# Value sums copied to SBUF before the softmax division, and the last stage's loads cut into paced pieces

## The chip, the cores and the metric

The kernel runs on one core of a Trainium2 chip. The metric is the device time of one execution in microseconds (us); three executions of the kernel before gave 1117.2, 1117.75 and 1119.46, so the median is 1117.75. Engines are called PE (TensorE), DVE (VectorE), ACT (ScalarE), POOL (GpSimd) and SP (SyncE, which issues all transfers here). PSUM is the memory that PE writes, in eight banks of 512 float32 columns; SBUF is the working memory.

## What is computed

One layer over a sequence of 2048 tokens of width 1024, batch 1, in bfloat16. Attention has 32 heads of width 32, and its result is multiplied, element by element, by a gate made from a two-layer network on the same normalized input.

```
xn  = layernorm(x)                                   # x: (1, 2048, 1024)
q, k, v = split(xn @ wqkv)                           # 32 heads of 32
p   = softmax(q @ k.T * 32 ** -0.5)                  # 2048 x 2048 per head
s   = concat_heads(p @ v) @ wo
y   = layernorm(xn)
g   = silu(gelu(y @ w1 + b1) @ w2 + b2)              # hidden width 3584
out = x + s * g
```

## The kernel before

The 32 heads are worked in eight groups of four (`HG = 8`), so that four heads fill the 128 partitions. Each group has eight blocks of 256 queries, and each block eight pairs of key tiles: 8 x 8 x 8 = 512 units of work. A unit (`unit`, line 921) is eight score matmuls on PE (line 932; one score group below), two exponentials of 128x1024 on ACT (line 941), the sum of the two key tiles on DVE (`PA`, line 944), and on PE eight small matmuls of the probabilities with V and four of `PA` with a tile of ones. The V products of a block gather in columns 0 to 255 of one PSUM bank and the softmax denominators in columns 256 to 511 of the same bank. `norm` (line 969) then divides: DVE transposes the denominators out of the bank (L971), takes reciprocals (L972), transposes these back and spreads them (L974), and multiplies the V sums, read from the bank, by them (L977). The bank is free for its next user after L977. Groups 0 to 6 write the result to a DRAM scratch (`o_scratch`, L1024); group 7 keeps it in `ot7`.

Everything else on PE is filler between the score groups, in four queues: `pro` (the first normalization and projections), `proj` (Q, K and V projections of the next group of heads), `mlp` (both layers of the network, whose weights stream in through rings of three `w1r` and four `w2r` tiles, L759 and L765, some 0.5 MB each), and `wo` (the output projection, one item for 128 tokens and 512 columns, eight matmuls over the eight head groups). The `wo` items need all heads: the seven stored groups come back from `o_scratch` into `big`, where the normalized input was (L997), and the weight `wo` goes where Q, K and the projection weights of finished groups were (L1000).

The order on every engine is made before launch by a planner (`_Plan.run`, line 78). It plays the program through with a cost for each instruction and gives each engine a fixed list; on the chip each engine follows its list and waits on semaphores. In the planner PE takes, at each free moment, the first of: a ready score group, the open V item, a filler item (`next_items`). A score group is put behind filler when the filler done so far lags the unit count (`paced`). A transfer costs its bytes at 210 GB/s behind all earlier ones, plus 1900 ns (`commit`, line 107). `proj` items fall due over 48 of the 64 units of a group.

So a piece of filler whose data the planner expects late is simply not in PE's list at that place, whether or not the data comes in time on the chip.

Line numbers of the changed kernel are 24 to 30 higher than those of the same code before (L932 is L956, L588 is L612, L765 is L789).

## Time and profile before

| what | value |
|---|---|
| median of 3 executions (lowest, highest) | 1117.75 us (1117.2, 1119.46) |
| profiled execution: its own time | 1117.59 us |
| its span, first to last instruction | 1115.4 us |
| busy: PE, ACT, DVE | 1038.8, 1034.9, 860.3 us |
| mean granted PE clock | 0.989 |

The profile gives for each engine how long it was busy. A PE row's end is modelled, and matmuls overlap, so a busy PE is not a PE at its peak. In a timeline row the first two numbers are start and length in us; the bracket gives the idle time of that engine just before, and which work ended it. A window row gives, for a stretch of the span, its length, the busy time of PE, of the weight loads (PEld), of DVE, ACT and POOL with the number of their instructions, then the granted PE clock (1.00 is full), the busy share of the DMA engines and their GB/s.

### The profile page before, as it was taken

The numbers are of one execution on the slowest core, as the hardware profiler recorded it, in microseconds if no ns is written. First come the engines' busy times: TensorE is split into PE (matmuls) and PEld (weight loads), VectorE is DVE, ScalarE is ACT, GpSimd is POOL, SyncE is SP. The second block draws the span as 40 slices with busy tenths as digits, with TensorE's granted clock in tenths as the row PEclk, the third lists the DMA queues.
The fourth block names the chain that finished last, engine by engine and source line by source line (L and its number), as shares of the span: only waits on it lengthen the run. The fifth ranks groups of instructions, "written<-read, shape, count | busy, mean of one in ns | idle before, by whom it ended". The sixth has DMA issues, their size and how long they took to land.

```text
span 1115.4 us, 34138 instructions
## 1 busy us (share of the span) xinstructions
PE 1038.8 (93%) x15238; PEld 669.1 (60%) x15305; DVE 860.3 (77%) x1570; ACT 1034.9 (93%) x1186; POOL 32.5 (3%) x42
## 2 busy tenths in 40 slices
PE   5898999999999899999999999999999997799997
PEld 4665476566766566557765666557666665466443
DVE  6699867787779776887779868976789777655775
ACT  4899989999999989999999999999999999868993
POOL 5600000000000000000000000000000000000000
PEclk9999999999999999999999999999999999799999
DMA  8345176233654356333574547333464547464333
GB/s 255 86 137 157 34 202 179 79 110 94 195 157 134 112 159 182 95 91 115 152 201 123 148 130 208 110 96 94 128 183 141 156 141 239 154 180 129 112 122 96
DMA packets 282380, 156.62 MB, mean 140 GB/s; under 512 B 23162, under 2 KB 271994, under 8 KB 282234
## 3 DMA queue, kind: packets, MB, share of 16 engines
q1 hardware_dynamic: 282234, 154.44, 47.9%
q8 instruction: 120, 1.97, 0.7%
q14 instruction: 26, 0.21, 0.1%
HBM read 142.35 MB, written 12.06 MB: 138 GB/s over the span
## 4 chain that ended last, share of the span: by engine, by line
ACT 57%; PE 37%; DVE 4%; POOL 1%; issue 1%; POOLq 0%; DMA 0%
ACT P L941 52%; PE ps L588 24%; PE ps L583 7%; PE ps L932 6%; ACT ut L815 3%; ACT gw L847 1%; POOL gw L724 1%; DVE PA L944 1%; DVE stats L710 0%; DVE nt L971 0%; DVE xb L807 0%; POOLq L1075 0%; ACT big L700 0%; DMA hT<-in_A_x_dram 0%; DVE hT L817 0%
## 5 line engine op out<-in xcount | busy, mean ns | idle before, releaser
L941 ACT ACTIVATE P<-ps 128x1024 bf16<-128x1024 f32 x1024 | 977.3, 1142 | 47.4 <-PE ps L932 44.9
L944 DVE TENSOR_TENSOR PA<-P 128x1024 bf16<-128x1024 bf16 x512 | 348.2, 688 | 134.7 <-ACT P L941 112.0
L588 PE MATMUL ps<-yT,w1r 128*128 128x256 bf16 x1792 | 232.3, 275 | 3.6 <-DVE xb L807 2.1
L588 PE MATMUL ps<-w2r,hT 128*128 128x256 bf16 x1792 | 224.6, 274 | 3.6 <-DVE hT L817 1.8
L588 PEld LDWEIGHTS ps<-yT,w1r 128*128 128x128 bf16 x1792 | 163.3, 98 | 60.3 <-issue 29.7
L588 PEld LDWEIGHTS ps<-w2r,hT 128*128 128x128 bf16 x1792 | 164.5, 98 | 52.1 <-issue 26.4
L583 PE MATMUL ps<-P,V 128*32 128x256 bf16 x4096 | 159.4, 276 | 0.8 <-DVE yT L1056 0.6
L588 PE MATMUL ps<-qk,big 128*128 128x256 bf16 (+1 forms) x718 | 120.3, 306 | 8.3 <-issue 1.9
L588 PE MATMUL ps<-big,qk 128*128 128x512 bf16 (+1 forms) x504 | 119.7, 367 | 8.5 <-issue 2.4
L932 PE MATMUL ps<-qk 32*128 32x256 bf16 x2048 | 102.3, 274 | 20.9 <-ACT P L941 19.8
L583 PE MATMUL ps<-PA,ones 128*32 128x256 bf16 x2048 | 118.0, 276 | 0.0
L932 PE MATMUL ps<-QKT 32*128 32x256 bf16 x2048 | 102.6, 275 | 16.1 <-ACT P L941 14.3
L583 PEld LDWEIGHTS ps<-P,V 128*32 128x32 bf16 x4096 | 102.0, 97 | 25.6 <-issue 9.5
L588 PEld LDWEIGHTS ps<-qk,big 128*128 128x128 bf16 x736 | 65.6, 98 | 48.4 <-issue 15.9
L815 ACT ACTIVATE ut<-ut 128x512 f32<-128x512 f32 x112 | 86.3, 773 | 2.9 <-DVE ut L813 2.9
L807 DVE TENSOR_TENSOR xb<-ps,b1T 128x512 bf16<-128x512 f32 x112 | 76.8, 685 | 15.6 <-PE ps L588 14.6
L817 DVE SCALAR_TENSOR_TENSOR hT<-ut,xb 128x512 bf16<-128x512 f32 x112 | 76.5, 684 | 8.4 <-ACT ut L815 8.3
L588 PEld LDWEIGHTS ps<-big,qk 128*128 128x128 bf16 x552 | 48.4, 99 | 57.1 <-issue 14.7
L932 PEld LDWEIGHTS ps<-qk 32*128 32x128 bf16 x2048 | 30.4, 92 | 84.4 <-ACT P L941 77.9
L932 PEld LDWEIGHTS ps<-QKT 32*128 32x128 bf16 x2048 | 30.4, 92 | 82.4 <-ACT P L941 75.3
L813 DVE SCALAR_TENSOR_TENSOR ut<-sq,xb 128x512 f32<-128x512 bf16 x112 | 76.9, 687 | 1.9
L583 PEld LDWEIGHTS ps<-PA,ones 128*32 128x32 bf16 x2048 | 53.1, 97 | 14.9 <-issue 13.3
(59 smaller groups left out, 460.6 us busy)
## 6 DMA issues: line engine op xcount, KB each, us to landing
w1r<-in_B_w_dram SPq DMA_DIRECT2D x112, 512.0 KB, 4.0
w2r<-in_B_w_dram SPq DMA_DIRECT2D x128, 448.0 KB, 4.3
qk<-in_A_wqkv_dram SPq DMA_DIRECT2D x16, 256.0 KB, 3.5
g_scratch<-gw SPq DMA_DIRECT2D x32, 128.0 KB, 2.7
o_scratch<-ot SPq DMA_DIRECT2D x56, 64.0 KB, 3.0
big<-o_scratch SPq DMA_DIRECT2D x7, 512.0 KB, 6.3
hT<-in_A_x_dram SPq DMA_DIRECT2D x10, 256.0 KB, 6.2
qk<-in_A_wqkv_dram SPq DMA_DIRECT2D x4, 512.0 KB, 4.3
```

The lines of the kernel that those rows point to most:

```text
L583: ins = e.matmul(dst(j), lhsT=lhsT(j), rhs=rhs(j), start=start, stop=stop, tile_position=(0, 32 * j), skip_group_check=True)
L588: return e.matmul(dst, lhsT=lhsT, rhs=rhs, start=start, stop=stop, skip_group_check=True)
L724: pool(lambda e, t=t: e.tensor_scalar(xnb[t % 4], xst[t], lnp[:, t, 1:2], lnp[:, t, 5:6], op0=ALU.mult, op1=ALU.add), 950, [XS(t), ("nb_", ...
L807: dve(lambda e: e.tensor_tensor(xb_t[i3][:].rearrange("p (k t) -> p k t", k=2), bank(it.bank).rearrange("p (k t) -> p k t", k=2), b1T[:, 2 ...
L813: dve(lambda e: e.scalar_tensor_tensor(ut_t[i3][:], sq_t[p % 2][:], 1.0 / GA, xb_t[i3][:], op0=ALU.add, op1=ALU.mult), c_f32(512), [("sq", ...
L815: act(lambda e: e.activation(ut_t[i3][:], ut_t[i3][:], ACT.Tanh, scale=GC * GA), c_act(512), [("ut", i3)], [("ut", i3)], 1)
L817: dve(lambda e: e.scalar_tensor_tensor(hT[:, hs].rearrange("p k t -> p (k t)"), ut_t[i3][:], 1.0, xb_t[i3][:], op0=ALU.add, op1=ALU.mult), ...
L847: act(lambda e: e.activation(zh_t[zi], z_t[zi], ACT.Tanh, scale=0.5), c_act(512), [("z", zi)], [("zh", zi)], 1)
L932: ins = e.matmul(bank(b0[j], kk * 256, (kk + 1) * 256), lhsT=QKT[sl][32 * j:32 * j + 32, 1, kb * 128:(kb + 1) * 128], rhs=QKT[sl][32 * j:3 ...
L941: x = act(lambda e, h=h: e.activation(P[pi][:, 2 * h:2 * h + 2].rearrange("p j k q -> p (j k q)"), ps[:, pr[h] * 1024:(pr[h] + 1) * 1024], ...
L944: pa = dve(lambda e: e.tensor_tensor(PA[ai][:], P[pi][:, :, 0, :], P[pi][:, :, 1, :], op=ALU.add), c_b16(1024), [("P", pi, 0), ("P", pi, 1 ...
```

## The change

Six edits go together.

- `norm` copies the V sums out of the bank into a new float32 tile `nv` (one more DVE instruction per block, 64 in all), right behind the transpose of the denominators, and multiplies from `nv`; the bank is free after this copy. Reciprocal, second transpose and product get a lower priority on DVE (2.2 in place of 1). To make room, the `PA` ring has seven tiles in place of eight.
- The seven transfers of 0.5 MB from `o_scratch` become 28 of 128 KB (seven groups by four quarters of the tokens); a quarter may start when its own quarter of the normalized input is no longer read.
- The one transfer of `wo` (2 MB) becomes eight of 256 KB, each waiting only for what lay in its place.
- These 36 pieces have the lowest priority in the planner and are issued only while its backlog of transfers is short; each is tied to the PE instruction that had last finished in the planner at that moment.
- The projections for the last group of heads fall due over 26 units in place of 48.
- `opens_at`: a filler item opens in the planner only when its later chunks will be ready too; a `wo` item only when all its data is planned.

```diff
--- before.py
+++ after.py
@@ -108,6 +108,11 @@
             e = o.eng
             o.start = t
             if e == "SP":
+                if o.prio >= 5:
+                    for x in reversed(order["PE"]):
+                        if x.fin <= t:
+                            o.deps[x] = True
+                            break
                 tf[e] = t + o.occ
                 state["bw"] = max(state["bw"], t) + o.nbytes / 210.0
                 o.fin = state["bw"] + 1900.0
@@ -137,6 +142,9 @@
                     pend[e].append(o)
             best = None
             bk = None
+            if e == "SP" and pend[e] and min(o.prio for o in pend[e]) >= 5 and state["bw"] > t + 1500:
+                wake(state["bw"] - 1400, e)
+                return None
             for o in pend[e]:
                 k = (o.prio, o.idx)
                 age = t - o.ready
@@ -188,6 +196,17 @@
             if pr is not None and "proj" not in out and (u >= pr.due - 12):
                 out.append("proj")
             return out
+
+        def opens_at(it, r):
+
+            off = 0.0
+            for c in it.chunks:
+                if c.left == 0:
+                    r = max(r, c.ready - off)
+                elif it.kind == "wo":
+                    return None
+                off += 1.2 * c.occ
+            return r
 
         def pe_step(t):
             cands = []
@@ -252,7 +271,10 @@
                             q.insert(heads["pro"], q.pop(k))
                         it = self.queues[n][heads[n]]
                         if it.chunks[0].left == 0:
-                            cands.append((max(bf[0], it.chunks[0].ready), 2, it.chunks[0], (it, bf[1], n)))
+                            r = opens_at(it, max(bf[0], it.chunks[0].ready))
+                            if r is None:
+                                continue
+                            cands.append((r, 2, it.chunks[0], (it, bf[1], n)))
                             if cands[-1][0] <= t:
                                 break
             best = None
...
-        NPA = 8
+        NPA = 7
...
-        ot7 = qk0[:, 8192:10240]
-        wo_sb = qk0[:, 0:8192].rearrange("p (c n) -> p c n", c=HG)
+        ot7 = qk0[:, 2048:4096]
+        wo_at = [4096, 5120, 6144, 7168, 8192, 9216, 0, 1024]
+        wo_sb = [qk0[:, a:a + 1024] for a in wo_at]
...
@@ -912,7 +936,7 @@
             if hg % 2 == 0:
                 lst += [("v", n) for n in range(NPR)]
             for k, (kind, t) in enumerate(lst):
-                due = 64 * w + 3 + int(k * 48 / len(lst))
+                due = 64 * w + 3 + int(k * (48 if w < 6 else 26) / len(lst))
                 if kind == "v":
                     plan.queues["proj"].append(v_item(hg // 2, t, "proj", due))
                 else:
@@ -969,13 +993,14 @@
         def norm(g, pv, ot_dst, W, extra=()):
             i = g % 2
             a = dve(lambda e: e.transpose(nt_t[i][:], bank(pv.bank, 256, 512)), c_ps(256), [], [("nt", i)], 1, pv)
+            dve(lambda e: e.tensor_copy(nv_t[i][:], bank(pv.bank, 0, 256)), c_ps(256), [], [("nv", i)], 1, pv)
             dve(lambda e: e.reciprocal(nr_t[i][:], nt_t[i][:].rearrange("p (b k) -> p b k", k=32)[:, :, 0]), 150,
-                [("nt", i)], [("nr", i)], 1)
+                [("nt", i)], [("nr", i)], 2.2)
             dve(lambda e: e.transpose(nb_t[i][:].rearrange("p (b k) -> p b k", k=32),
                                       nr_t[i][:].unsqueeze(2).to_broadcast([128, 8, 32])), c_f32(256),
-                [("nr", i)], [("nb", i)], 1)
-            return dve(lambda e: e.tensor_tensor(ot_dst, bank(pv.bank, 0, 256), nb_t[i][:], op=ALU.mult), c_ps(256),
-                       [("nb", i)], W, 1, pv, extra)
+                [("nr", i)], [("nb", i)], 2.2)
+            return dve(lambda e: e.tensor_tensor(ot_dst, nv_t[i][:], nb_t[i][:], op=ALU.mult), c_f32(256),
+                       [("nb", i), ("nv", i)], W, 2.2, None, extra)
 
         OTr = xnT
         for tq in range(1, 4):
@@ -985,20 +1010,25 @@
                 proj(w + 1, w)
             else:
 
-                dead = []
-                for t in range(NT):
-                    for d in [plan.last_w[("xnT", t)]] + plan.readers[("xnT", t)]:
-                        if d not in dead:
-                            dead.append(d)
-                wdead_ = [("Q", 0, n) for n in range(NPR)] + [("K", 0, n) for n in range(NPR)] + \
-                        [("wqk", i) for i in range(3)] + [("wv",)]
-                dead7 = [d for d in [plan.last_w[("wv",)]] + plan.readers[("wv",)]]
-                for hg in range(HG - 1):
-                    dma(f"otl{hg}", lambda e, hg=hg: e.dma_start(OTr[:, hg, :], o_d[hg]), 524288,
-                        [("o_d", hg, q) for q in range(NQB)], [("OTr", hg)], extra=dead)
-                wdead = [t for t in wdead_]
-                dma("wo", lambda e: e.dma_start(wo_sb, A_wo.rearrange("(c p) n -> p c n", p=128)), 2097152, [],
-                    wdead + [("wo",)])
+                def over(toks):
+                    ops = []
+                    for t in toks:
+                        for d in [plan.last_w.get(t)] + plan.readers.get(t, []):
+                            if d is not None and d not in ops:
+                                ops.append(d)
+                    return ops
+                dead7 = over([("K", 0, n) for n in range(NPR)])
+                for qt in range(4):
+                    dead = over([("xnT", t) for t in range(4 * qt, 4 * qt + 4)])
+                    for hg in range(HG - 1):
+                        dma(f"otl{hg}{qt}", lambda e, hg=hg, qt=qt: e.dma_start(OTr[:, hg, qt * 512:(qt + 1) * 512],
+                                                                          o_d[hg, :, qt * 512:(qt + 1) * 512]), 131072,
+                            [("o_d", hg, 2 * qt), ("o_d", hg, 2 * qt + 1)], [("OTr", hg, qt)], 5, dead)
+                    for hc in (2 * qt, 2 * qt + 1):
+                        wd = over([[("wqk", 0)], [("wqk", 1)], [("wqk", 2)], [("wv",)], [("wv",)], [],
+                                   [("Q", 0, n) for n in range(NPR)], [("Q", 0, n) for n in range(NPR)]][hc])
+                        dma(f"wo{hc}", lambda e, hc=hc: e.dma_start(wo_sb[hc], A_wo[hc * 128:(hc + 1) * 128, :]), 262144, [],
+                            [("wo", hc)], 5, wd)
             for qb in range(NQB):
                 g = w * NQB + qb
                 pv = _Item("pv")
```

The changed lists, at three places. First PE at the start of the last group of heads. `QKT` or `qk` to `ps` at 128x256 x8 is one score group (x24 is three in a row with nothing between), `yT,w1r` is the first layer, `w2r,hT` the second, `qk,big` at 128x512 the output projection or a projection. Before, from score group 450:

```order
L932 MATMUL ps<-QKT 128x256 x8
L588 MATMUL ps<-yT,w1r 128x256 x8
L932 MATMUL ps<-QKT 128x256 x8
L588 MATMUL ps<-yT,w1r 128x256 x8
L932 MATMUL ps<-QKT 128x256 x24
L588 MATMUL ps<-qk,big 128x512 x6
L932 MATMUL ps<-QKT 128x256 x24
L583 MATMUL ps<-P,V 32x256 x32
```

and a little later, from the end of the next V item on (the first row), with score groups 458 and 459:

```order
L583 MATMUL ps<-PA,ones 32x256 x16
L932 MATMUL ps<-QKT 128x256 x8
L588 MATMUL ps<-qk,big 128x512
L932 MATMUL ps<-QKT 128x256 x8
L588 MATMUL ps<-qk 128x512
L588 MATMUL ps<-yT,w1r 128x256 x16
L588 MATMUL ps<-w2r,hT 128x256 x56
```

Now, from score group 452:

```order
L956 MATMUL ps<-QKT 128x256 x8
L612 MATMUL ps<-w2r,hT 128x256 x12
L956 MATMUL ps<-QKT 128x256 x8
L612 MATMUL ps<-w2r,hT 128x256 x6
L956 MATMUL ps<-QKT 128x256 x8
L612 MATMUL ps<-w2r,hT 128x256 x12
L956 MATMUL ps<-QKT 128x256 x8
L612 MATMUL ps<-w2r,hT 128x256 x12
L956 MATMUL ps<-QKT 128x256 x8
L612 MATMUL ps<-w2r,hT 128x256 x14
L956 MATMUL ps<-QKT 128x256 x8
L612 MATMUL ps<-w2r,hT 128x256 x9
```

Before, three score groups stand in a row twice, and 73 filler matmuls in a row follow; now each score group is followed by 6 to 14 filler matmuls.

Second, PE early in the program. Before, from score group 35:

```order
L932 MATMUL ps<-qk 128x256 x8
L583 MATMUL ps<-PA,ones 32x256 x12
L588 MATMUL ps<-dg,onesf 128x128 x2
L932 MATMUL ps<-qk 128x256 x8
L588 MATMUL ps<-big,qk 128x512 x9
L932 MATMUL ps<-qk 128x256 x8
L588 MATMUL ps<-big,qk 128x512 x9
L932 MATMUL ps<-qk 128x256 x8
L588 MATMUL ps<-big,qk 128x512 x6
L932 MATMUL ps<-qk 128x256 x8
L588 MATMUL ps<-big,qk 128x512 x9
```

Now, from score group 35:

```order
L956 MATMUL ps<-qk 128x256 x8
L607 MATMUL ps<-PA,ones 32x256 x8
L607 MATMUL ps<-P,ones 32x256 x8
L612 MATMUL ps<-w2r,hT 128x256 x42
L956 MATMUL ps<-qk 128x256 x8
L612 MATMUL ps<-w2r,hT 128x256 x4
L956 MATMUL ps<-qk 128x256 x24
L612 MATMUL ps<-w2r,hT 128x256 x10
L956 MATMUL ps<-qk 128x256 x8
L612 MATMUL ps<-big,qk 128x512 x6
L956 MATMUL ps<-qk 128x256 x8
L612 MATMUL ps<-big,qk 128x512 x7
```

Projections that stood between score groups 36 and 39 come later, 42 matmuls of the second layer stand in one row behind group 35, and groups 37 and 38 have nothing behind them.

Third, SP where the stored heads come back. Before:

```order
L759 DMA w1r<-in_B_w_dram 128x8x256 x2
L997 DMA big<-o_scratch 128x2048 x6
L765 DMA w2r<-in_B_w_dram 128x7x256 x3
L1024 DMA o_scratch<-ot 128x256
L765 DMA w2r<-in_B_w_dram 128x7x256
L759 DMA w1r<-in_B_w_dram 128x8x256 x2
L850 DMA g_scratch<-gw 128x2x256
L759 DMA w1r<-in_B_w_dram 128x8x256
L1024 DMA o_scratch<-ot 128x256
```

Now (L1024 is a 128 KB piece of the stored heads, L1030 a 256 KB piece of `wo`, L783 and L789 the two layers' weights):

```order
L783 DMA w1r<-in_B_w_dram 128x8x256
L789 DMA w2r<-in_B_w_dram 128x7x256 x3
L1054 DMA o_scratch<-ot 128x256
L789 DMA w2r<-in_B_w_dram 128x7x256
L1024 DMA big<-o_scratch 128x512 x6
L874 DMA g_scratch<-gw 128x2x256
L1024 DMA big<-o_scratch 128x512 x11
L783 DMA w1r<-in_B_w_dram 128x8x256
L1054 DMA o_scratch<-ot 128x256
L1030 DMA qk<-in_A_wo_dram 128x1024
L1024 DMA big<-o_scratch 128x512
L783 DMA w1r<-in_B_w_dram 128x8x256
```

Six pieces of 0.5 MB that stood in a row are now 17 of 128 KB at this place, of which each waits for a PE instruction; the rest stand singly between the weights.

7 lines of the change are left out of this document (4 added, 3 removed).

## The prediction

> **What bounds the kernel now.** First the page's busy times.
>
> ```profile
> PE 1038.8 (93%) x15238; PEld 669.1 (60%) x15305; DVE 860.3 (77%) x1570; ACT 1034.9 (93%) x1186; POOL 32.5 (3%) x42
> ACT  4899989999999989999999999999999999868993
> ```
>
> PE and ACT tie at 93%, so the share decides nothing. The groups of instructions show who waits for whom.
>
> ```profile
> L941 ACT ACTIVATE P<-ps 128x1024 bf16<-128x1024 f32 x1024 | 977.3, 1142 | 47.4 <-PE ps L932 44.9
> L932 PEld LDWEIGHTS ps<-qk 32*128 32x128 bf16 x2048 | 30.4, 92 | 84.4 <-ACT P L941 77.9
> ```
>
> The score matmuls wait for ACT again and again, 77.9 us at one of their two tiles alone, and ACT waits for PE 44.9 us in all. So the exponentials set the pace, and a loss is an idle stretch of ACT. Next, the stretches.
>
> ```profile
> 600.00:700.00 100.00, 98.04 (x1532) 65.03 (x1536) 81.03 (x146) 99.49 (x117) 0.00 (x0) 1.00 0.54 153
> 940.00:960.00 20.00, 14.55 (x248) 9.19 (x237) 13.66 (x25) 17.41 (x21) 0.00 (x0) 0.83 0.33 97
> 980.00:1000.00 20.00, 18.71 (x201) 13.53 (x196) 11.24 (x20) 13.04 (x15) 0.00 (x0) 0.98 0.66 192
> ```
>
> In the middle ACT (fourth busy number) is busy 99.49 of 100 us; between 940 and 1000 it isn't, and the PE clock falls to 0.83 on the mean. So I read the ACT timeline for every gap. Those from 905 to 1020:
>
> ```profile
> 908.50 1.94 ACT L941 ACTIVATE P<-ps 128x1024 bf16<-128x1024 f32 x2 [1.58 <-PE ps L932]
> 952.28 1.94 ACT L941 ACTIVATE P<-ps 128x1024 bf16<-128x1024 f32 x2 [1.61 <-PE ps L932]
> 954.74 3.77 ACT L941 ACTIVATE P<-ps 128x1024 bf16<-128x1024 f32 x4 [0.53 <-PE ps L932]
> 961.07 5.63 ACT L941 ACTIVATE P<-ps 128x1024 bf16<-128x1024 f32 x6 [1.53 <-PE ps L932]
> 972.06 5.61 ACT L941 ACTIVATE P<-ps 128x1024 bf16<-128x1024 f32 x6 [0.68 <-PE ps L932]
> 981.29 3.77 ACT L941 ACTIVATE P<-ps 128x1024 bf16<-128x1024 f32 x4 [3.63 <-PE ps L932]
> 987.26 0.63 ACT L815 ACTIVATE ut<-ut 128x512 f32<-128x512 f32 x1 [2.19 <-DVE ut L813]
> 991.34 3.77 ACT L941 ACTIVATE P<-ps 128x1024 bf16<-128x1024 f32 x4 [3.45 <-PE ps L932]
> 1014.75 3.77 ACT L941 ACTIVATE P<-ps 128x1024 bf16<-128x1024 f32 x4 [3.62 <-PE ps L932]
> ```
>
> They sum to 18.8 us. The price of a long block of filler between two score groups can be read too:
>
> ```profile
> 139.01 0.40 PE L932 MATMUL ps<-qk 32*128 32x256 bf16 x8
> 146.44 0.40 PE L932 MATMUL ps<-qk 32*128 32x256 bf16 x8
> 1008.52 0.40 PE L932 MATMUL ps<-QKT 32*128 32x256 bf16 x8
> 1008.85 5.52 PE L588 MATMUL ps<-w2r,hT 128*128 128x256 bf16 x49
> 1014.30 0.40 PE L932 MATMUL ps<-QKT 32*128 32x256 bf16 x8
> ```
>
> Score groups 5.78 us apart (1008.52, 1014.30) cost ACT 3.62 us at 1014.75, a difference of 2.16; those 7.43 apart (139.01, 146.44) cost 5.32 at 146.89 (row below), a difference of 2.11. So idle ACT = spacing less 2.1. A matmul of 256 columns takes (1014.30 - 1008.85) / 49 = 0.111 us in a block, and a score group 0.33 until the next work.
>
> **The change part by part.** *A, the stored heads and `wo` in pieces, earlier projections.* Before, PE's list there has score groups with nothing between them, then blocks of 73 and 49; the planner had the weights queued behind 5.5 MB. On the chip PE then ran thin, and its clock went:
>
> ```profile
> 940.80:944.20 3.40, 1.36 (x40) 0.52 (x28) 3.24 (x7) 3.40 (x6) 0.00 (x0) 1.00 0.11 33
> 944.20:947.60 3.40, 0.72 (x10) 0.23 (x10) 2.00 (x4) 3.40 (x6) 0.00 (x0) 0.89 0.00 0
> 947.60:951.00 3.40, 3.03 (x20) 1.88 (x21) 0.81 (x2) 3.06 (x4) 0.00 (x0) 0.50 0.00 0
> ```
>
> A window with PE busy 1.36 of 3.40 us kept the full clock; one with 0.72 was followed by half clock. In the new order no score group from 308 to 507 has a block of more than some 2.5 us behind it, by counts times 0.111, and none stands bare. So the thin stretch, the half clock and the blocks go together. The 36 pieces move the same 5.5 MB. Of the 18.8 us I leave 1.5 for waits that no list shows (bounds: 0, and half, 9.4, if the pieces come late). A = -17.3.
>
> *B, the middle.* Three gaps stand there:
>
> ```profile
> 383.61 3.77 ACT L941 ACTIVATE P<-ps 128x1024 bf16<-128x1024 f32 x4 [1.95 <-PE ps L932]
> 410.21 3.77 ACT L941 ACTIVATE P<-ps 128x1024 bf16<-128x1024 f32 x4 [2.97 <-PE ps L932]
> 510.23 3.77 ACT L941 ACTIVATE P<-ps 128x1024 bf16<-128x1024 f32 x4 [2.37 <-PE ps L932]
> ```
>
> 7.3 us; the last two lie behind 31 and 38 second-layer matmuls in a row. The new order has one such block from group 58 on, 31 matmuls behind group 307: spacing 0.33 + 31 x 0.111 = 3.8, idle 1.7. B = -5.6 (bounds -7.3 and 0).
>
> *C, the early order.* Since `norm` differs, the planner's list parts from the old one at the first block of queries. Before:
>
> ```profile
> 109.14 3.77 ACT L941 ACTIVATE P<-ps 128x1024 bf16<-128x1024 f32 x4 [0.69 <-PE ps L583]
> 126.14 5.61 ACT L941 ACTIVATE P<-ps 128x1024 bf16<-128x1024 f32 x6 [0.70 <-PE ps L583]
> 132.30 9.27 ACT L941 ACTIVATE P<-ps 128x1024 bf16<-128x1024 f32 x10 [0.56 <-PE ps L932]
> 146.89 3.77 ACT L941 ACTIVATE P<-ps 128x1024 bf16<-128x1024 f32 x4 [5.32 <-PE ps L932]
> 956.76 2.73 PE ps L583 x96
> ```
>
> 7.3 us. The last row is a V item of 96 small matmuls run in one go, 2.73 us. Now: group 35 has 16 small ones (16/96 of 2.73, 0.46) and 42 large (4.66), spacing 5.45, idle 3.3; group 42 a V item and three matmuls of 512 columns (twice 0.111 each, 0.67), spacing 3.7, idle 1.6; group 57 a V item and 42 large, spacing 7.7, idle 5.6; the 0.7 at 109.14 stays. That is 11.2. Behind group 35 stand groups 36 to 38 with four filler matmuls in all: three units of some 1.9 us (four exponentials take 3.77), so 5.6 us with PE busy about 1.4, as thin as the window that lost its clock. The gap at 383.61 is one such loss, 1.95; I take 2.0 (bounds 0, and 4.3, the 0.68 and 3.63 at 972.06 and 981.29 where the clock stayed low longer). C = 11.2 + 2.0 - 7.3 = +5.9.
>
> The Trainium skill, "TensorE: Matmul & The Clock Gate", "Part 1: The HAM clock gate", has the clock fall to half after an idle window of about 3.4 us. Read strictly, groups 36 to 38 leave no idle window, the 2.0 would be nothing, and the sum 1099.5. The window with 0.72 us of work speaks against the strict reading.
>
> *D, the end.*
>
> ```profile
> 1085.85 3.77 ACT L941 ACTIVATE P<-ps 128x1024 bf16<-128x1024 f32 x4 [1.00 <-PE ps L932]
> 1090.06 1.94 ACT L941 ACTIVATE P<-ps 128x1024 bf16<-128x1024 f32 x2 [0.43 <-PE ps L932]
> 1093.29 5.61 ACT L941 ACTIVATE P<-ps 128x1024 bf16<-128x1024 f32 x6 [1.29 <-PE ps L932]
> ```
>
> 2.7 us, with uneven blocks from group 506 on; the new order is even there, I leave half, 1.3. Behind the last exponential both orders have the same one matmul and six groups of eight of the output projection, so that tail stays, but the last block's copy stands ahead of its division: one copy, 0.4 (next fence). D = -1.0 (bounds -2.7 and +0.4).
>
> *E, the copy.* The trace has the same shape, 128x256 float32 out of PSUM:
>
> ```profile
> L785 DVE COPY sbc<-ps 128x256 f32<-128x256 f32 x8 | 3.3, 411 | 0.0
> L977 DVE TENSOR_TENSOR ot<-ps,nb 128x256 bf16<-128x256 f32 x56 | 23.5, 420 | 1.4
> 610.00:620.00 10.00, 9.65 (x170) 6.51 (x173) 10.00 (x19) 10.00 (x14) 0.00 (x0) 1.00 0.50 138
> ```
>
> 64 x 0.411 = 26.3 us more on DVE, 860 to 887 of some 1100. The product from SBUF has no row; I take L977's 0.42 for it. The cover is DVE's own idle time: the unit's sum waits for ACT, and at 610 to 620 DVE was busy all 10.00 us while ACT, too, was busy 10.00. In such stretches what the copy delays is PA, behind it the product with ones on PE and the bank; PE's ones stand three units behind, over 5 us. For it, the bank comes free after transpose and copy instead of four operations. I take +2.0 (bounds -1 and the whole 26.3 were there no cover). The Trainium skill, "VectorE: DVE Perf Modes", "Rules for kernel authors", advises the copy out of PSUM only where many operations follow; here one does, so by it the copy is pure work, 26.3 us on DVE, which the trace's idle DVE covers. `PA` with seven tiles for eight is nothing as long as PE's ones stand three units behind.
>
> *Sum:* -17.3 - 5.6 + 5.9 - 1.0 + 2.0 = -16.0, against the profiled execution's 1117.59 (span 1115.4 and 2.2 around it; the median is 1117.75): **1101.6 us**.
>
> **The rivals.** *R1, the pieces hold SP.* Each piece waits for a PE instruction, and SP works in order: behind a waiting piece stand weight loads, and for these PE's filler waits. For it:
>
> ```profile
> big<-o_scratch SPq DMA_DIRECT2D x7, 512.0 KB, 6.3
> g_scratch<-gw SPq DMA_DIRECT2D x32, 128.0 KB, 2.7
> ```
>
> 128 KB take 2.7 us to land and 512 KB 6.3, so four pieces one after the other cost 10.8 for 6.3. Against it: the weights wait for PE themselves, and pieces overlap. Half of A's 18.8 stays: 1101.6 + 9.4 - 1.5 = 1109.5. The Trainium skill, "DMA: Bandwidth & Descriptors", "Bandwidth", asks for transfers of 1 MiB or more and so speaks for this rival; the two rows agree with it, 47 KB per us against 81.
>
> *R2, the early place costs more:* clock low for as long as at 967 to 981, and a longer gap at group 57; 2.3 more for the clock and 2 for the gap, 1105.9. For it, the bare groups; against, one such place only.
>
> *R3, the stretch stays:* PE waits there for weights or bank in another form and C eats the rest: 1117.6. Against it, the 99.49 in the middle with the same ring of weights.
>
> *R4, DVE becomes the bound (slower).* Place: stretches like 610 to 620, where DVE has nothing idle. If the copies land on ACT's path, up to 26.3 in place of 2.0: 1101.6 + 24.3 = 1125.9; it decides from 18.0 of the 26.3, about 70% exposed. Against it, the copy is one in 16 us.
>
> **How the numbers follow.** A measurement of this kernel tells 0.2%, 2.2 us, from no change. Forecast 0.66, R1 0.13, R2 0.11, R3 0.04, R4 0.06. Forecast, R1 and R2 are faster: 0.90; R3 is the same, 0.04; R4 slower, 0.06. The low end takes all of A's gain (-1.5), no clock loss (-2.0), no cost of E and its gain (-3.0) and half of D's remainder (-0.6): 1094.5, so 1094. The high end takes in R1 and 2 more, 1112.
>
> **What would show it.** Right: ACT busy above 19 of 20 us in each stretch from 900 to 1080, clock 1.00 there; ACT gaps of about 3, 1.6 and 5.6 us between 100 and 170, half clock once at about 120; one gap of 1.7 near 660; DVE busy some 887. Wrong: PE waits on transfers or half clock after 900 (A, R1); many small ACT gaps that end on PE waiting for DVE (E, R4); no half clock early (C).

## The result, and the profile after

| what | before | changed |
|---|---|---|
| median of 4 executions each (lowest, highest) | 1117.47 us (1116.7, 1119.46) | 1090.95 us (1090.77, 1091.3) |
| profiled execution: its time, its span | 1117.59, 1115.4 us | 1091.05, 1088.9 us |
| busy: PE, ACT, DVE | 1038.8, 1034.9, 860.3 us | 1044.3, 1032.5, 858.1 us |
| mean granted PE clock | 0.989 | 0.996 |

The ratio is 0.976 with the interval 0.9743 to 0.9777: 26.5 us less, where 16.0 were forecast. The direction was right, and the time lies 3 us below the low end of the range.

From the page of the changed kernel, its busy times, the 40 slices of ACT, and the two groups that the prediction began with (`L965` was `L941`, `L956` was `L932`):

```profile
PE 1044.3 (96%) x15309; PEld 665.7 (61%) x15309; DVE 858.1 (79%) x1633; ACT 1032.5 (95%) x1186; POOL 32.5 (3%) x42
ACT  4799798999999999999999999999999999999993
L965 ACT ACTIVATE P<-ps 128x1024 bf16<-128x1024 f32 x1024 | 979.5, 1170 | 25.2 <-PE ps L956 22.5
L956 PEld LDWEIGHTS ps<-qk 32*128 32x128 bf16 x2048 | 30.4, 92 | 76.6 <-ACT P L965 71.0
```

The dip to 8, 6, 8 near the end of ACT's row has gone, and a dip to 7, 9, 8 stands in slices 5 to 7. The idle time ahead of the exponentials fell from 47.4 to 25.2 us, and the score groups still wait for ACT (71.0 at one tile). The exponentials set the pace in both kernels, so ACT's idle time is the account to keep. Here it is by stretch, up to the end of the last exponential; the columns are those of the window rows shown ahead. First the kernel before:

```profile
100.00:200.00 100.00, 94.38 (x1384) 60.16 (x1388) 75.70 (x136) 92.31 (x108) 0.00 (x0) 1.00 0.51 143
200.00:900.00 700.00, 674.33 (x10192) 443.38 (x10221) 561.37 (x1002) 690.25 (x798) 0.00 (x0) 1.00 0.47 135
900.00:1020.00 120.00, 103.42 (x1461) 67.61 (x1468) 77.61 (x136) 101.14 (x118) 0.00 (x0) 0.91 0.63 187
1020.00:1098.90 78.90, 74.29 (x1068) 34.90 (x1078) 56.16 (x104) 75.57 (x82) 0.00 (x0) 1.00 0.34 107
```

Then the changed kernel:

```profile
100.00:200.00 100.00, 93.76 (x1278) 57.94 (x1277) 72.53 (x133) 88.23 (x103) 0.00 (x0) 0.97 0.49 136
200.00:900.00 700.00, 690.11 (x10405) 449.02 (x10398) 565.59 (x1055) 697.66 (x808) 0.00 (x0) 1.00 0.50 142
900.00:1020.00 120.00, 115.05 (x1777) 73.00 (x1775) 89.13 (x169) 119.10 (x138) 0.00 (x0) 1.00 0.55 160
1020.00:1072.43 52.43, 52.21 (x712) 22.48 (x710) 40.51 (x78) 51.91 (x57) 0.00 (x0) 1.00 0.43 132
```

Length less ACT's busy time (the fourth busy number) is its idle time:

| stretch, and the prediction's term | before | changed | difference | forecast |
|---|---|---|---|---|
| 100 to 200 (C) | 7.69 | 11.77 | +4.1 | +5.9 |
| 200 to 900 (B) | 9.75 | 2.34 | -7.4 | -5.6 |
| 900 to 1020 (A) | 18.86 | 0.90 | -18.0 | -17.3 |
| 1020 to the last exponential (D) | 3.33 | 0.52 | -2.8 | -1.4 |
| behind it (D) | 16.5 | 16.5 | 0 | +0.4 |
| the copy (E) | | | no gap of its own | +2.0 |
| ACT's own busy time | 1034.9 | 1032.5 | -2.4 | not in the sum |

They sum to -26.5, the fall of the span from 1115.4 to 1088.9; that they do is arithmetic, since the span is ACT's idle time, its busy time and what stands behind it. (The first 100 us are alike, 23.7 and 23.6 idle.)

The predicted marks, in ACT's timeline of the changed kernel:

```profile
116.43 4.69 ACT L965 ACTIVATE P<-ps 128x1024 bf16<-128x1024 f32 x5 [1.33 <-PE ps L956]
125.32 1.94 ACT L965 ACTIVATE P<-ps 128x1024 bf16<-128x1024 f32 x2 [0.94 <-PE ps L956]
128.47 1.94 ACT L965 ACTIVATE P<-ps 128x1024 bf16<-128x1024 f32 x2 [1.22 <-PE ps L956]
168.16 3.77 ACT L965 ACTIVATE P<-ps 128x1024 bf16<-128x1024 f32 x4 [4.66 <-PE ps L956]
667.03 3.77 ACT L965 ACTIVATE P<-ps 128x1024 bf16<-128x1024 f32 x4 [1.57 <-PE ps L956]
```

The block at group 57 cost 4.66 (5.6 forecast), the one behind group 307 1.57 (1.7). The block behind group 35 cost 2.3 in two gaps, 0.97 and the 1.33 of the first row, with 3.3 forecast. At groups 57 and 35 the spacing of the score groups was near the forecast (7.86 and 5.57 us in PE's timeline, for 7.7 and 5.45), but ACT had two `ut` operations of 0.6 to 0.7 us each to do in that time. Between 116 and 135 stand the bare groups, and the clock went there once, as forecast for "about 120":

```profile
114.42:117.84 3.42, 3.06 (x35) 1.68 (x33) 3.10 (x7) 2.04 (x3) 0.00 (x0) 1.00 0.88 246
117.84:121.25 3.41, 0.54 (x16) 0.20 (x16) 1.38 (x2) 3.41 (x5) 0.00 (x0) 1.00 0.55 164
121.25:124.66 3.41, 2.63 (x19) 1.39 (x20) 1.38 (x2) 3.13 (x4) 0.00 (x0) 0.52 0.00 0
124.66:128.08 3.42, 3.42 (x23) 1.00 (x22) 1.29 (x2) 1.94 (x2) 0.00 (x0) 0.50 0.47 139
```

A window with PE busy 0.54 of 3.41 us is followed by two at half clock, 6.8 us in all. After 900 the clock stays full up to the last exponential.

### The profile page after: what moved, and what is told of

Its sections match the earlier page's. It is cut to its first block, busy times and chain, and to the rows that moved or that the text cites. A ratio compares the mean times of both kernels' runs of the same rounds, so it can differ in the third digit from the quotient of the medians.

```text
span 1088.9 us, 34312 instructions
## 1 busy us (share of the span) xinstructions
PE 1044.3 (96%) x15309; PEld 665.7 (61%) x15309; DVE 858.1 (79%) x1633; ACT 1032.5 (95%) x1186; POOL 32.5 (3%) x42
## 4 chain that ended last, share of the span: by engine, by line
ACT 64%; PE 31%; DVE 3%; POOL 1%; DMA 1%; issue 0%; POOLq 0%
ACT P L965 59%; PE ps L612 20%; PE ps L607 6%; PE ps L956 5%; ACT ut L839 4%; ACT gw L871 1%; POOL gw L748 1%; DVE stats L734 0%; DVE PA L968 0%; DMA w1r<-in_B_w_dram 0%; DVE hT L841 0%; POOLq L1105 0%; ACT big L724 0%; DMA hT<-in_A_x_dram 0%; DVE xb L831 0%
## 5 line engine op out<-in xcount | busy, mean ns | idle before, releaser
L965 ACT ACTIVATE P<-ps 128x1024 bf16<-128x1024 f32 x1024 | 979.5, 1170 | 25.2 <-PE ps L956 22.5
L968 DVE TENSOR_TENSOR PA<-P 128x1024 bf16<-128x1024 bf16 x511 | 343.8, 684 | 113.8 <-ACT P L965 61.0
L612 PE MATMUL ps<-big,qk 128*128 128x512 bf16 (+1 forms) x552 | 133.6, 372 | 1.7 <-ACT big L724 1.1
L612 PE MATMUL ps<-qk,big 128*128 128x256 bf16 (+1 forms) x736 | 124.7, 306 | 4.7 <-ACT big L724 1.8
L956 PE MATMUL ps<-qk 32*128 32x256 bf16 x2048 | 102.1, 274 | 11.6 <-ACT P L965 10.4
L956 PE MATMUL ps<-QKT 32*128 32x256 bf16 x2048 | 101.7, 273 | 4.3 <-ACT P L965 4.2
L839 ACT ACTIVATE ut<-ut 128x512 f32<-128x512 f32 x112 | 89.0, 805 | 1.0 <-DVE ut L837 1.0
L956 PEld LDWEIGHTS ps<-qk 32*128 32x128 bf16 x2048 | 30.4, 92 | 76.6 <-ACT P L965 71.0
L956 PEld LDWEIGHTS ps<-QKT 32*128 32x128 bf16 x2048 | 30.3, 92 | 71.0 <-ACT P L965 66.1
```

The source lines that it names most:

```text
L612: return e.matmul(dst, lhsT=lhsT, rhs=rhs, start=start, stop=stop, skip_group_check=True)
L839: act(lambda e: e.activation(ut_t[i3][:], ut_t[i3][:], ACT.Tanh, scale=GC * GA), c_act(512), [("ut", i3)], [("ut", i3)], 1)
L956: ins = e.matmul(bank(b0[j], kk * 256, (kk + 1) * 256), lhsT=QKT[sl][32 * j:32 * j + 32, 1, kb * 128:(kb + 1) * 128], rhs=QKT[sl][32 * j:3 ...
L965: x = act(lambda e, h=h: e.activation(P[pi][:, 2 * h:2 * h + 2].rearrange("p j k q -> p (j k q)"), ps[:, pr[h] * 1024:(pr[h] + 1) * 1024], ...
L968: pa = dve(lambda e: e.tensor_tensor(PA[ai][:], P[pi][:, :, 0, :], P[pi][:, :, 1, :], op=ALU.add), c_b16(1024), [("P", pi, 0), ("P", pi, 1 ...
```

## The experiments

The theory that I tested, called L, is that the time follows the planner's fixed lists: blocks of filler between score groups, and bare groups that cost the clock. The rivals put the gain into what the chip does with the same lists: the bank that comes free sooner, transfers that land sooner. In three sets the kernels of a set shared a chip and its runs of the kernel before: the copy alone, the loads alone, and the two held lists of 1117.74; the kernel without `opens_at`, the unpaced one, the seven tiles and the ramp of 1118.46; the doubled copy, the 48 units, the old priority and the slack of 18 of 1119.55. So across sets the ratios are compared.

**The copy alone.** The kernel before with the changed `norm` and seven `PA` tiles.

```diff
-        NPA = 8
+        NPA = 7
...
+        nv_t = [sb(f"nv{i}", [128, 256], F32) for i in range(2)]
...
+            dve(lambda e: e.tensor_copy(nv_t[i][:], bank(pv.bank, 0, 256)), c_ps(256), [], [("nv", i)], 1, pv)
...
-                [("nt", i)], [("nr", i)], 1)
+                [("nt", i)], [("nr", i)], 2.2)
...
+            return dve(lambda e: e.tensor_tensor(ot_dst, nv_t[i][:], nb_t[i][:], op=ALU.mult), c_f32(256),
+                       [("nb", i), ("nv", i)], W, 2.2, None, extra)
```

> The kernel before with the copy in norm alone (new priorities, seven PA tiles); loads as before. Theory L (the time follows the lists: a block of filler between two score groups costs ACT its spacing less some 2.1 us, bare score groups cost the PE clock): the middle of the list is as in the changed kernel (one block of 31 left), the early place too, but the bare groups and the blocks of 73 and 46 at groups 443 to 469 are back. The changed kernel lost 7.4 us less idle ACT at 200 to 900 us and 4.1 more at 100 to 200, so 1117.5 - 3.3 - some 1 for fewer interruptions of ACT = 1113, between 1110 and 1116. Theory H (the bank that is free earlier is worth time by itself on the chip, the 10 us that the forecast missed): 1107 or less.

Measured 1106.67 us, ratio 0.9904 (0.9891 to 0.9918): 11.1 us less, where L expected 4.5; the number is in the range of rival H. The windows show where it arose:

```profile
200.00:900.00 700.00, 687.97 (x10393) 449.03 (x10392) 564.71 (x1054) 697.65 (x809) 0.00 (x0) 1.00 0.49 137
900.00:1090.00 190.00, 176.10 (x2508) 98.89 (x2510) 131.88 (x248) 172.45 (x194) 0.00 (x0) 0.95 0.52 157
```

The middle has 2.35 us of idle ACT, the same as in the whole change: B belongs to the copy's edit. The late stretch keeps 17.55 of the 22.2 that the kernel before has from 900 on, and half clock: A doesn't. L had counted all of the late stretch as kept. Of what went there, 2.6 us are D (0.75 idle behind 1020 for 3.33), which so belongs to the copy's edit too. Whether list or bank is the cause is left to the held lists below.

**The loads alone.** The changed kernel with the old `norm` and eight `PA` tiles.

```diff
-        NPA = 7
+        NPA = 8
...
-            dve(lambda e: e.tensor_copy(nv_t[i][:], bank(pv.bank, 0, 256)), c_ps(256), [], [("nv", i)], 1, pv)
...
-            return dve(lambda e: e.tensor_tensor(ot_dst, nv_t[i][:], nb_t[i][:], op=ALU.mult), c_f32(256),
-                       [("nb", i), ("nv", i)], W, 2.2, None, extra)
+            return dve(lambda e: e.tensor_tensor(ot_dst, bank(pv.bank, 0, 256), nb_t[i][:], op=ALU.mult), c_ps(256),
+                       [("nb", i)], W, 1, pv, extra)
```

> The changed kernel with the old norm (product read from PSUM, old priorities, eight PA tiles): pieces, pacing, opens_at and the earlier projections alone. Theory L: the list up to group 400 is the old one, with its blocks at 49, 178, 227, and the last stage is smooth but for 3.9 us at 409: of the 20.8 us idle ACT that went after 900 us some 19 go, 1117.5 - 19 = 1098.5, between 1096 and 1101; no half clock after 900 us. Theory H: the loads give only what was forecast for them, 17.3, and the rest needs the copy: 1100 or more. The two differ little here; the run is for the sum of the parts: with L the two parts add up to the whole, 26.5, within some 3 us.

Measured 1104.66 us (1100.74 to 1104.94), ratio 0.9874 (0.9855 to 0.9892): 13.1 us less, against some 19 expected; this number, too, is in rival H's range. The late stretch gives what A promised, the middle has 11.7 us idle for 9.75 before, and an early loss is new:

```profile
200.00:900.00 700.00, 679.19 (x10263) 441.45 (x10252) 559.30 (x997) 688.29 (x795) 0.00 (x0) 1.00 0.49 139
900.00:1020.00 120.00, 115.16 (x1725) 75.81 (x1724) 90.40 (x160) 118.50 (x139) 0.00 (x0) 1.00 0.59 169
93.24 1.94 ACT L964 ACTIVATE P<-ps 128x1024 bf16<-128x1024 f32 x2 [1.82 <-PE ps L606]
112.78 3.77 ACT L964 ACTIVATE P<-ps 128x1024 bf16<-128x1024 f32 x4 [1.88 <-PE ps L606]
```

The two timeline rows are gaps behind two half clocks of 3.4 us each, which began at 88.4 and 108.9. One execution of four took 1100.74, some 4 us less than the others, with a mean granted clock of 0.998 for their 0.995; the profile of that one isn't there, so that it lacked this loss is likely and not shown. The two parts give 11.1 and 13.1, together 24.2 of the 26.5: nearly a plain sum.

**The copy in held lists.** To price the copy without a new plan, the old lists were kept on PE, ACT and SP, and the copy was put in the transpose's place in DVE's list. In one kernel the bank waits for the product as before; in the other, for the copy (groups 0 to 6).

```diff
-            a = dve(lambda e: e.transpose(nt_t[i][:], bank(pv.bank, 256, 512)), c_ps(256), [], [("nt", i)], 1, pv)
+            def tc(e):
+                e.transpose(nt_t[i][:], bank(pv.bank, 256, 512))
+                return e.tensor_copy(nv_t[0][:], bank(pv.bank, 0, 256))
+            a = dve(tc, c_ps(256), [], [("nt", i), ("nv", 0)], 1, pv)
...
+        for o in plan.ops:
+            if o.eng == "PE":
+                for d in [d for d in o.deps if d in early]:
+                    del o.deps[d]
+                    o.deps[early[d]] = True
```

(The last five lines are in the second kernel only.)

> The lists of the kernel before, held instruction for instruction on PE, ACT and SP; on DVE each first transpose is followed by the copy to one SBUF tile and the product reads that tile, but PE still waits for the product before it uses the bank. So this is the price of 64 copies by themselves, 26 us of DVE. Theory L and the forecast's cover: 0 to +2 us, 1117.5 to 1119.5. Rival R4 (DVE becomes the bound): 18 us or more slower, 1135 and up.

> As the kernel with the copies and the old lists, but PE's next user of the bank waits for the copy and not for the product (head groups 0 to 6): the early release by itself, some 1 us earlier 56 times, with the lists held. Theory L: PE's list puts other work there anyway, within 1 us of the kernel that waits for the product. Theory H: 5 us or more faster than that one.

Measured 1123.98 us, ratio 1.0059 (1.0046 to 1.0071), and 1123.44, ratio 1.0056 (1.0044 to 1.0069). So 64 copies cost 6.2 us, not 0 to 2, and the early release gives 0.5 of it back, which these runs can't tell from nothing. In the old lists, then, the bank's early release on the chip is worth next to nothing, and the middle keeps its idle time (11.1 us with early release, for 9.75 in the kernel before and 2.35 with the copy's own list). What the copy alone gained came with the other list that the planner makes when it knows of that release. Whether that new list would keep its gain if the bank came free late on the chip wasn't tried. The price shows in PE's waits. The kernel before:

```profile
PEld ps L588 <- DVE xb L807: 8.0, 15, 1.1
PE ps L588 <- DVE xb L807: 3.7, 9, 0.6
PEld ps L583 <- DVE PA L944: 2.1, 8, 0.4
```

The held list with early release:

```profile
PEld ps L589 <- DVE xb L808: 10.7, 15, 1.3
PE ps L589 <- DVE xb L808: 6.6, 11, 1.0
PEld ps L584 <- DVE PA L945: 2.1, 8, 0.4
```

`xb` (L807 before) is the copy of the first layer's sums out of their bank, which PE needs back. PE's waits for it grew by 2.7 and 2.9 us, 5.6 in all, while its wait for `PA` stayed at 2.1. That 5.6 is near the 5.7 lost is chance: a PE wait needn't reach ACT, and in this profile (5.9 us longer) ACT's idle time grew by 3.7 us only, while its own busy time grew by 1.9, from 1034.9 to 1036.7, and 0.3 stand behind the last exponential. In the first kernel's profile 3.6 us of the loss are idle ACT in the first 100 us, with a half clock at 89.8.

**The copy twice in the changed lists.** The changed kernel's lists were held and the copy made a second time into a spare tile, ahead of the first.

```diff
+        dup = sb("dup", [128, 256], F32)
...
-            dve(lambda e: e.tensor_copy(nv_t[i][:], bank(pv.bank, 0, 256)), c_ps(256), [], [("nv", i)], 1, pv)
+            def two(e):
+                e.tensor_copy(dup[:], bank(pv.bank, 0, 256))
+                return e.tensor_copy(nv_t[i][:], bank(pv.bank, 0, 256))
+            dve(two, c_ps(256), [], [("nv", i)], 1, pv)
```

> The changed kernel's lists, held instruction for instruction on PE, ACT and SP; on DVE each of the 64 copies is made twice, the first time into a spare tile, so PE gets the bank 0.4 us later and DVE has 26 us more to do. The price of the copy in the new lists. Theory L with the cover of the forecast (DVE's idle time hides it): 0 to +2 us, 1091 to 1093. Theory P (the copy costs some 6 us with any list held, as it did with the old lists, and the changed kernel gains 6 us more elsewhere to pay for it): +4 to +8, 1095 to 1099.

Measured 1097.7 us, ratio 0.9808 (0.9794 to 0.9823) against the changed kernel's 0.976: 0.0048 of 1119.55, 5.4 us more. In other lists, with DVE's order made for one copy, another costs about the same. Of the profile's 6.2 us, 2.7 are again ACT's own busy time (1035.2 for 1032.5); most of the rest is idle time between 200 and 900 (4.5 for 2.3). Here the waits name the copy itself. The changed kernel:

```profile
PEld ps L612 <- DVE nv L996: 9.0, 22, 0.9
PE ps L612 <- DVE nv L996: 1.3, 5, 0.4
```

With two copies:

```profile
PEld ps L613 <- DVE nv L1000: 18.1, 27, 1.2
PE ps L613 <- DVE nv L1000: 6.9, 15, 0.7
```

PE's filler stands at the bank for 10.3 us in the changed kernel and for 25.0 with the second copy.

**Without `opens_at`.** The changed kernel, in which an item opens when its first chunk is ready.

```diff
-                            r = opens_at(it, max(bf[0], it.chunks[0].ready))
-                            if r is None:
-                                continue
-                            cands.append((r, 2, it.chunks[0], (it, bf[1], n)))
+                            cands.append((max(bf[0], it.chunks[0].ready), 2, it.chunks[0], (it, bf[1], n)))
```

> The changed kernel without opens_at: an item of filler opens in the planner as soon as its first chunk is ready. Theory L (the time follows the lists): eight places in PE's list from group 443 to 455 are bare again, a block of some 19 us stands behind group 459 and one of 5.2 behind 465; 17 + 3 us of idle ACT and half clock on top, so 1091 + 22 = 1113, between 1108 and 1118, no better than the kernel before by much. Rival S (the small pieces by themselves bring the gain, since the weights come between them): within 3 us of the changed kernel, 1088 to 1094.

Measured 1113.84 us, ratio 0.9947 (0.993 to 0.9963), as L expected: without it the pieces do little, and the late stretch is thin again.

```profile
900.00:1020.00 120.00, 98.34 (x1412) 64.04 (x1410) 75.74 (x139) 96.68 (x113) 0.00 (x0) 0.89 0.51 149
935.80:939.20 3.40, 0.79 (x16) 0.24 (x16) 2.99 (x9) 3.40 (x5) 0.00 (x0) 1.00 0.00 0
939.30:952.95 13.65, 8.05 (x136) 4.26 (x136) 4.57 (x7) 10.74 (x12) 0.00 (x0) 0.50 0.15 44
952.95:956.30 3.35, 1.23 (x25) 0.33 (x17) 2.24 (x6) 2.47 (x3) 0.00 (x0) 1.00 0.34 98
956.30:969.95 13.65, 7.10 (x116) 3.51 (x120) 4.99 (x8) 12.30 (x14) 0.00 (x0) 0.50 0.11 31
```

ACT is idle 23.3 of 120 us, and twice a window with PE busy a quarter or a third is followed by 13.65 us at half clock. So A needs the rule that PE's list is not opened for an item whose later data comes late. Whether this rule would do it without the pieces wasn't tried.

**Without pacing.** The 36 pieces at an ordinary priority, not tied to PE and not held for the backlog.

```diff
-                if o.prio >= 5:
-                    for x in reversed(order["PE"]):
...
-            if e == "SP" and pend[e] and min(o.prio for o in pend[e]) >= 5 and state["bw"] > t + 1500:
...
-                            [("o_d", hg, 2 * qt), ("o_d", hg, 2 * qt + 1)], [("OTr", hg, qt)], 5, dead)
+                            [("o_d", hg, 2 * qt), ("o_d", hg, 2 * qt + 1)], [("OTr", hg, qt)], 3, dead)
...
```

> The changed kernel with its 36 pieces, but without their pacing: normal priority, no tie to a PE instruction, issued as soon as their place is free. The list of PE differs in one place, a block of 4.8 us behind group 459. Theory L: 2.7 us more idle ACT and some more, 1093.5, between 1091 and 1096. Rival R1 of the forecast turned around (pacing is what keeps the weights coming on the chip): 1098 or more, with PE waiting on transfers after 900 us.

Measured 1093.61 us, ratio 0.9768 (0.9754 to 0.9783); the interval overlaps the changed kernel's. Its late stretch:

```profile
900.00:1020.00 120.00, 113.59 (x1721) 72.52 (x1717) 86.39 (x164) 115.28 (x134) 0.00 (x0) 0.97 0.53 151
```

4.7 us of ACT are idle there for 0.9. That is 3.8 more, where the one changed block in PE's list was expected to cost 2.7; in the whole time pacing can't be told from nothing.

**The last projections over 48 units, as before.**

```diff
-                due = 64 * w + 3 + int(k * (48 if w < 6 else 26) / len(lst))
+                due = 64 * w + 3 + int(k * 48 / len(lst))
```

> The changed kernel with the last projections due over 48 units as before. Theory L: one more block, 3.6 us behind group 459, 1.4 us by the count: 1092.5, between 1090.5 and 1094.5. Rival W (the pieces need the earlier projections; without these they come when the weights do): 1097 or more.

Measured 1093.75 us, ratio 0.9768 (0.975 to 0.9783): at most a us or two, not told from nothing either.

**The old priority on DVE.**

```diff
-                [("nt", i)], [("nr", i)], 2.2)
+                [("nt", i)], [("nr", i)], 1)
...
-                       [("nb", i), ("nv", i)], W, 2.2, None, extra)
+                       [("nb", i), ("nv", i)], W, 1, None, extra)
```

> The changed kernel with the old priority (1) for reciprocal, second transpose and product. Theory L: by the count of blocks 17.7 us against 12.3, three thin places instead of one, so 1091 + 5.4 = 1096.5, between 1094 and 1100. Theory Q (the lower priority is no more than order on DVE, and DVE isn't the bound): within 2 us, 1089 to 1093.

Measured 1100.12 us, ratio 0.983 (0.9815 to 0.9845): 7.8 us more than the changed kernel, at the outer edge of what L expected. A number by which the planner orders DVE's work is worth more than the copy's price.

**Seven `PA` tiles alone.** The kernel before with one number changed.

```diff
-        NPA = 8
+        NPA = 7
```

> The kernel before with seven PA tiles in place of eight and nothing else. The changed kernel pays for room with this. Theory L: the lists part from the old ones and get more blocks (by my count of spacing less 2.1 us, 39.1 us against 30.9), so 8 us slower, 1126, between 1121 and 1130. Rival T (one tile less is nothing, as the forecast had it, as PE's ones stand three units behind): within 2 us of the kernel before.

Measured 1125.84 us, ratio 1.0058 (1.0042 to 1.0074): 6.5 us slower. The forecast had this at nothing. ACT's timeline of its profiled execution (1121.93 us, the fastest of its eight) has, in the middle, gaps that the kernel before hasn't or has smaller:

```profile
278.75 3.77 ACT L941 ACTIVATE P<-ps 128x1024 bf16<-128x1024 f32 x4 [2.54 <-PE ps L932]
511.41 3.77 ACT L941 ACTIVATE P<-ps 128x1024 bf16<-128x1024 f32 x4 [3.13 <-PE ps L932]
674.11 3.77 ACT L941 ACTIVATE P<-ps 128x1024 bf16<-128x1024 f32 x4 [2.34 <-PE ps L932]
```

Before there was nothing near the first, 2.37 at the second and 0.51 at the third, so these three hold 5.1 us more. ACT waits there for scores that stand behind filler in PE's list. Two of the eight executions took 1122 us at a mean clock of 0.994 or 0.995, the other six 1125.6 to 1127.1 at 0.987 to 0.990; what these six lost beyond, some 4 us, comes with the clock, and no profile shows where. Its list differs from the first block of queries on; this piece of the difference shows how:

```order
 L932 MATMUL ps<-qk 128x256 x16
-L588 MATMUL ps<-yT,w1r 128x256 x16
-L932 MATMUL ps<-qk 128x256 x8
-L583 MATMUL ps<-P,V 32x256 x32
...
+L588 MATMUL ps<-yT,w1r 128x256 x14
+L583 MATMUL ps<-P,V 32x256 x16
+L932 MATMUL ps<-qk 128x256 x8
+L583 MATMUL ps<-P,V 32x256 x16
```

Every later choice of the planner follows from another state.

**More slack.** The planner holds a score group behind filler when the filler lags by more than the slack, in units; 10 was raised to 18 in the changed kernel.

```diff
-        plan.run(HG * 64, 10)
+        plan.run(HG * 64, 18)
```

> The changed kernel with the filler allowed to lag by 18 units in place of 10 throughout. Theory L: blocks by the count 4.7 us against 12.3, and no bare group (so no early half clock, 2), but 8.0 us more PE work (36 matmuls of 512 columns) behind the last score group: 1091 - 7.6 - 2 + 8 = 1089.5, between 1087 and 1092. Rival M (blocks cost less than counted, the tail its full price): 1094 or more.

Measured 1092.89 us, ratio 0.9767 (0.9752 to 0.9782), no difference from the changed kernel and no decision between the two theories. Its windows:

```profile
100.00:200.00 100.00, 94.58 (x1361) 55.91 (x1366) 78.90 (x146) 97.34 (x113) 0.00 (x0) 0.98 0.42 118
200.00:900.00 700.00, 682.32 (x10334) 448.39 (x10367) 561.59 (x1048) 692.77 (x801) 0.00 (x0) 1.00 0.51 143
```

From 100 to 200 ACT is busy for 9.1 us more than in the changed kernel, in the middle it gives back 4.9, and behind the last exponential, where L had put 8.0 us of PE work, 23.9 us stand for 16.5.

**Slack on a ramp.** Slack 16, falling to 10 between units 256 and 480, one `nv` tile, eight `PA` tiles.

```diff
-                            state["done"] < dense_total * (state["s"] - dense_slack) / total_units:
+                            state["done"] < dense_total * (state["s"] - 16 + 6 * min(1.0, max(0.0, (state["s"] - 256) / 224.0))) / total_units:
...
-        NPA = 7
+        NPA = 8
...
-        nv_t = [sb(f"nv{i}", [128, 256], F32) for i in range(2)]
+        nv_t = [sb(f"nv{i}", [128, 256], F32) for i in range(1)]
...
```

> The changed kernel with one nv tile and eight PA tiles, and with the slack by which filler may lag at 16 units up to unit 256, falling to 10 at unit 480 (10 throughout before). Theory L: blocks of 4.2, 3.3, 3.4 and 3.2 us are left in PE's list, 7.5 us by the count against 12.3 in the changed kernel, no bare group, so no half clock early, the same tail behind the last score group: 1091 - 4.8 - 2 = 1084, between 1081 and 1088. Rival M (what is left at 100 to 200 us is the chip's, not the list's): 1089 or more.

Measured **1082.52 us** (1082.18 to 1082.85), ratio 0.9671 (0.9656 to 0.9685), faster than both kernels. Its windows:

```profile
100.00:200.00 100.00, 96.83 (x1395) 58.24 (x1393) 80.10 (x149) 98.31 (x115) 0.00 (x0) 1.00 0.45 125
900.00:1020.00 120.00, 116.02 (x1699) 71.66 (x1701) 90.81 (x170) 117.52 (x135) 0.00 (x0) 1.00 0.56 162
```

Against the changed kernel the early stretch has 10.1 us more of ACT, and the late one 1.6 less; by the ratios it is 9.9 us faster. So C, the largest loss that the forecast saw in the change, was a matter of the list too, and can be had back; which of the three numbers does it wasn't tried.

## Where the prediction was right, and the step that failed

**What bounds the kernel: right.** 24.1 of the 26.5 us are idle time of ACT that went, and the score groups still wait for ACT (71.0 us at one tile).

**A, right in size and partly in cause.** -18.0 for -17.3, and the loads alone bring it (118.50 of 120 busy). The thin stretch and the half clock came and went together: from 900 to 1020 the mean granted clock was 0.89 to 0.97 in every profile with more than 4 us of idle ACT there, and 0.99 or 1.00 in all others. The forecast counted this on the new list, so it could get the size without the cause. The prediction's heading for it named the pieces and earlier projections, though. With these and the copy's edit, but without `opens_at`, the kernel is 0.5% faster than before (ratio 0.9947), less than with the copy's edit alone (0.9904); so A doesn't come without the rule that opens an item.

**B, right, undersized.** -7.4 for -5.6: three gaps were listed, 7.3 of the 9.75 idle; smaller ones went too. The cause is the copy's edit, through the list: with the copy in the old lists next to nothing of this went (9.25 and 11.1 us idle for 9.75).

**C, right in kind, oversized.** +4.1 for +5.9. The blocks at groups 35 to 42, the clock loss there, and group 57 stand where they were forecast. The sum of the nine early gaps was 11.6 for 13.2. The two large blocks cost 4.66 and 2.3 for 5.6 and 3.3: "idle ACT = spacing less 2.1" was taken from two blocks in which ACT had nothing else to do, and here it did two `ut` operations in each.

**D, undersized.** The uneven blocks of the end nearly went whole (-2.8 of 3.3), and the copy ahead of the last division doesn't show: 16.5 us behind the last exponential in both. (With the old lists held it did, 16.8.)

**E, wrong in its mechanism.** The prediction said "what the copy delays is PA", "I take +2.0", and that seven tiles for eight are "nothing". In held lists the copy costs 5.4 to 6.2 us, near 0.09 for each on the mean, and seven tiles cost 6.5 with a new plan. In the old lists PE's wait for `PA` didn't grow (2.1 us in both); its waits for the DVE work that gives a bank back to the filler did, there and with the second copy. Yet with both edits and the lower priority the kernel is 11.1 us faster than without, since the planner makes another list. Price and gain come through two doors, what DVE does and what the planner believes, and the forecast had one. In the changed kernel the price has no gap of its own; it can only lie inside what remains in the other rows. The Trainium skill, "VectorE: DVE Perf Modes", "Rules for kernel authors", advises such a copy only before many operations; the two held lists agree with it on the chip's side (5.4 and 6.2 us lost).

**The step that failed: the sum and its low end.** The sum had no term for ACT's own busy time, put at nothing without a reason, and it took B's and D's gain from the listed gaps alone. ACT's own busy time fell by 2.4 us. Two timeline rows of the changed kernel show a part of it:

```profile
101.91 1.94 ACT L965 ACTIVATE P<-ps 128x1024 bf16<-128x1024 f32 x2
104.25 1.03 ACT L965 ACTIVATE P<-ps 128x1024 bf16<-128x1024 f32 x1
```

One exponential takes 1.03, two 1.94, four 3.77: the first of a chain adds 0.1 us more than those behind it. ACT's timeline shows 45 gaps before and 30 now, so 15 chains fewer are about 1.5 us (an estimate from these rows). The rest isn't assigned.

The 10.5 us between forecast and account are C 1.8, B 1.8, A 0.7, D 1.8, E 2.0 and ACT 2.4: six small misses, all in one direction. The range's low end let A, D, E and C's clock loss move but held B and C's blocks fixed, and had no row for ACT itself. Set beside that low end (1094.5), A gave 0.8 less than it granted, C 0.2 and E 1.0; B gave 1.8 more, D 1.2 and ACT's busy time 2.4. So the time fell out of the range by B, D and ACT's busy time. E didn't bring it there: its price, mis-sized, points the other way, and the list that paid for it is in the rows of B and D. (A slip besides: without the 2.0 of clock loss the sum is 1099.6, not 1099.5.)

**The rivals.** R1 (pieces hold SP) fell: transfers of 128 KB landed in 3.0 us as the median, and nothing of the late stretch stayed.

```profile
big<-o_scratch SPq DMA_DIRECT2D x28, 128.0 KB, 3.0
```

The Trainium skill, "DMA: Bandwidth & Descriptors", "Bandwidth", would have 1 MiB or more for each transfer, to come near peak bandwidth; here smaller ones cost nothing that shows. R2 (the early place costs more) came at less than the forecast's own value, not more. R3 fell with A. R4 (DVE becomes the bound) fell: ACT is busy 697.66 of 700 us in the middle, and DVE's busy time is 858.1, not the 887 forecast, since instructions right behind one another overlap (the busy times of all DVE groups sum to 922.7 us before and 940.4 after, while DVE's own stays). That is the new order's doing: in the old lists 64 copies took DVE's busy time to 876.3 and 876.8, some 0.25 us for each. What held lists lose, 6 of the 26 us, is a quarter of R4's price at most, and that it arises by R4's mechanism isn't shown.

## What to carry to other kernels

Where a planner fixes the lists, ask of each edit two things apart: what it costs on the chip with the lists held, and what list it gives; one number (a ring's size, a priority, a slack) can move more than the work that was added, in either direction. To price an added instruction, hold the lists and double it. When losses are summed from listed gaps, count the idle time of the whole stretch first: the small gaps that no one lists can go with the large ones, and here all misses had the same sign. Give the busy time of the engine that sets the pace a term too.
